# Attention and gated MLP on one core: low parts and reciprocals move to GpSimd, v without zero padding, the value product in three parts

## The chip, the cores and the metric

The kernel runs on one core of a Trainium2 chip. A core has TensorE (PE in the profile; its weight loads are PEld), VectorE (DVE), ScalarE (ACT), GpSimd (POOL) and SyncE (SP), which issues most DMAs. Each engine works through its own instructions in order and waits for others by semaphores. The metric is the device time of one execution in microseconds (us), the median of three runs.

## The reference

```python
# attention: q, k, v are (8, 12, 448, 64)
q_n, k_n = rmsnorm(q, g_q), rmsnorm(k, g_k)          # over the 64 of a head
scores = q_n @ k_n.T / sqrt(64)
attn = exp(scores - max(scores)); attn /= attn.sum(-1) + 1e-9
x = (attn @ v), heads joined: (8, 448, 768)
# gated MLP
h = gelu_tanh(x @ w_in)                              # (8, 448, 1024)
u, v2 = h[..., :512], h[..., 512:]
v_n = (v2 - mean) / sqrt(var + 1e-6) * g_ln          # over the 512
v_s = w_sg @ v_n + b_sg[:, None]                     # over the 448 positions
out = x + (u * v_s) @ w_out
```

## The kernel before

A number is carried through TensorE as two 16-bit halves, a high part and a low part (value minus high part), and a product is three matmuls: high by high, high by low, low by high. So for every operand someone makes the low part by a subtract.

The 96 heads of the 8 batches are taken in 48 pairs, and two pairs make a unit (24 units). The 448 positions are 3.5 tiles of 128, so a unit of two pairs has 7 tiles of queries; the middle one holds the last 64 positions of the first pair in its lower partitions and those of the second pair in its upper ones. The loop at the end of the kernel goes over the pairs. In each turn it prepares the next unit's q and k (squares, `norms`, `split`), makes the halves of this pair's v (`vsplit`), and then draws from generators in turn, by quotas: `scores` of the unit (quota SC), `pv` of the pair before (quota SV), the weights' preparation in the first 12 turns (quota WR), and `moe`, the MLP of the batch before (M0, M1, MR, ML). What a generator emits before it yields gets a place in the program; a scheduler then orders every engine's instructions from these places and its own estimate of times.

- `scores` (L409): per tile, TensorE makes the scores in PSUM (L423), DVE the negated row maximum (`nm`, L426), ACT two exponentials with row sums into the SBUF tile `ex` (L429), ACT the high part (L432) and DVE the low part (L433) of `ahl`, and SP transposes `ahl` into `at` by DMA (L438). After the middle and the last tile it calls `recips` (L380), which makes the reciprocals of the sums in two halves: four DVE instructions on 8 columns (`rx` L387, `ry` L388, `rh` L389, `rl` L390).
- `pv` (L445): `recip_row` (L392) spreads the reciprocals into a row by TensorE (L403), ACT copies it out (L406); then the value product is made in PSUM (L454, L459), DVE multiplies by the row (L461), ACT and DVE make the halves of x (L464, L465). The row and the product share one PSUM buffer.
- v is loaded for three pairs at once (`load_v`, L302, from SP's queue) into one of two buffers. The buffer has eight columns of 64 per pair, of which one half of two columns is zero, so that the step of the middle tile, 64 positions of either head, can be done by full 128x128 matmuls. `vsplit` makes the high part on ACT (L374) and the low part on DVE in one fused instruction, scale and subtract (L375).
- `split` (L327): GpSimd multiplies q and k by their weights and norms and subtracts for the low part (L334, L335, L340). In `moe` GpSimd gates (`gt`, L619) and makes low parts (`gl`, `gtl`).
- `weights` (L162): w_in and w_out come as 64-bit numbers and are decoded on DVE, ACT and GpSimd; DVE makes their low parts (L201, L247).
- `moe` (L488): `mv` and `mu` are the two halves of x @ w_in, `ms` is the product with w_sg, `mo` the one with w_out and the sum with x. `ms` is done for two feature tiles at a time (L601 to L624).

## Time and profile before

| | us |
|---|---|
| three runs | 1021.99, 1025.98, 1031.14; median 1025.98 |
| profiled execution | 1023.31, its span 1021.5 |
| DVE busy | 801.4 |
| ACT busy | 739.6 |
| GpSimd busy | 385.4 |
| PE busy by records | 826.5 |

Busy time is the time in which an engine has at least one instruction in work. Matmul records overlap, since the next one starts before the last has ended, so a busy PE has room left. The chain of work that ended last is followed back from the last instruction, at each step to what released it; its shares tell where the time was decided. An instruction's row names its line, operation, result and operands, its number, busy time and mean, and behind that the idle time of its engine in front of it and who ended it.

### The profile page before, as it was taken

Reading aid. Unit: us, or ns where it says so; the run is one execution under the profiler, and the core shown is the slowest. Engines: PE = TensorE matmul, PEld = TensorE weight load, DVE = VectorE, ACT = ScalarE, POOL = GpSimd, SP = SyncE. Lnnn points to the kernel's source line nnn. Section 1 sums busy time; section 2 is a strip of 40 time slices with the busy share of each in tenths; the row PEclk is TensorE's granted clock in tenths of the full one; section 3 lists DMA queues with packets and bytes.
Section 4 is the critical chain, followed back from the end, with each engine's and each line's share of the span. In section 5 each row is a group of like instructions: output and inputs, shape, how many; then the busy total and the mean of one; then the engine's idle time right before and its main releaser. Section 6 shows DMA issues by size and latency. Waiting matters only on the chain.

```text
span 1021.5 us, 16315 instructions
## 1 busy us (share of the span) xinstructions
PE 826.5 (81%) x5700; PEld 423.3 (41%) x5700; DVE 801.4 (78%) x1476; ACT 739.6 (72%) x1449; POOL 385.4 (38%) x263
## 2 busy tenths in 40 slices
PE   0324467737788899789897999989997899999998
PEld 0111224312553346344453455434643365445546
DVE  5699998999979977888789977887789768776140
ACT  2766798766777878686886877688778877786241
POOL 1465820436734362341543146322453253004021
PEclk9986678868989999899999899999998999999999
DMA  6977677776498869786789749793797676844102
GB/s 158 229 197 174 143 179 164 170 171 120 114 189 192 183 137 194 162 202 127 136 202 190 169 105 200 177 206 84 161 203 167 126 149 158 163 91 102 36 1 63
DMA packets 448002, 155.68 MB, mean 152 GB/s; under 512 B 404336, under 2 KB 441776, under 8 KB 447920
## 3 DMA queue, kind: packets, MB, share of 16 engines
q1 hardware_dynamic: 447344, 154.18, 69.3%
q8 instruction: 45, 0.74, 0.3%
q10 hardware_dynamic: 576, 0.46, 0.2%
q14 instruction: 37, 0.30, 0.1%
HBM read 43.57 MB, written 11.01 MB: 53 GB/s over the span
## 4 chain that ended last, share of the span: by engine, by line
DVE 31%; PE 28%; ACT 16%; DMA 10%; issue 9%; POOL 3%; SPq 3%; ACTq 0%; DVEq 0%; POOLq 0%
DVE ahl L433 8%; DMA at<-ahl 5%; DVE nm L426 5%; ACT ex L429 5%; ACT ahl L432 3%; PE s L423 3%; PE pv L459 3%; DVE vl L375 2%; DMA vr<-in_v_dram 2%; DVE ss L314 2%; DVE vl L568 1%; ACT sqv L358 1%; DVE pv L461 1%; DMA raw<-in_moe_w_in_dram 1%; SPq L302 1%
## 5 line engine op out<-in xcount | busy, mean ns | idle before, releaser
L429 ACT ACTIVATE ex<-s,nm 128x448 f32<-128x448 f32 x336 | 209.4, 631 | 76.8 <-DVE nm L426 51.6
L433 DVE TENSOR_TENSOR ahl<-ex,ahl 128x896 f16<-128x896 f32 x168 | 213.4, 1272 | 56.8 <-ACT ahl L432 55.4
L423 PE MATMUL s<-qt 64*128 64x448 f16 (+1 forms) x1152 | 156.9, 389 | 88.7 <-ACT ex L429 62.4
L426 DVE TENSOR_REDUCE nm<-s 128x2 f32<-128x896 f32 x168 | 180.8, 1081 | 18.4 <-PE s L423 18.2
L432 ACT ACTIVATE ahl<-ex 128x896 f16<-128x896 f32 x168 | 159.7, 951 | 37.8 <-DMA at<-ahl 35.8
L335 POOL TENSOR_TENSOR qk<-qk,ny 128x896 f32<-128x896 f32 x46 | 85.7, 1885 | 139.1 <-DVE ny L125 109.2
L619 POOL TENSOR_TENSOR gt<-gt,u 128x448 f32<-128x448 f32 x32 | 39.1, 1224 | 239.8 <-DVE gt L618 181.7
L340 POOL TENSOR_TENSOR hl<-qk,hl 128x896 f16<-128x896 f32 x46 | 94.6, 2070 | 69.9 <-ACT hl L339 69.7
L423 PEld LDWEIGHTS <-qt 64*128 64x128 f16 (+1 forms) x1152 | 49.2, 102 | 163.9 <-issue 102.8
L459 PE MATMUL pv<-at,vh 128*64 128x448 f16 x576 | 91.8, 371 | 0.0
L580 PEld LDWEIGHTS <-wi 128*128 128x128 f16 x576 | 57.6, 104 | 72.6 <-issue 31.3
L334 POOL TENSOR_TENSOR qk<-qk,gg 128x896 f32<-128x896 f32 x23 | 50.2, 2181 | 80.4 <-ACT sqk L313 78.2
L403 PE MATMUL row<-ident_h,rh 128*64 128x128 f16 (+1 forms) x384 | 36.6, 241 | 39.9 <-DVE xl L465 30.4
L429 ACT ACTIVATION_READ_ACCUMULATOR ex<-s,nm 128x1 f32 x336 | 67.8, 202 | 0.0
L314 DVE TENSOR_REDUCE ss<-sqk 128x14 f32<-128x896 f32 x48 | 51.6, 1076 | 17.6 <-ACT sqk L313 17.6
L313 ACT ACTIVATE sqk<-qk 128x896 f32<-128x896 f32 x48 | 45.6, 951 | 18.6 <-DVE ss L314 10.3
L339 ACT ACTIVATE hl<-qk 128x896 f16<-128x896 f32 x48 | 44.6, 945 | 13.6 <-POOL qk L335 6.9
L459 PE MATMUL pv<-at,vl 128*64 128x448 f16 x288 | 53.2, 367 | 0.0
L375 DVE SCALAR_TENSOR_TENSOR vl<-vr,v_s,vh 128x512 f16<-128x512 f32 x48 | 49.7, 1039 | 1.3 <-ACT vh L374 1.0
L459 PEld LDWEIGHTS <-vh 128*64 128x64 f16 x576 | 33.7, 114 | 40.5 <-issue 23.4
L403 PEld LDWEIGHTS <-rh 128*64 128x64 f16 (+1 forms) x384 | 22.5, 117 | 61.9 <-DVE xl L465 34.6
L522 PEld LDWEIGHTS <-xh 128*128 128x128 f16 x288 | 25.9, 99 | 46.8 <-issue 13.0
(1100 smaller groups left out, 2063.7 us busy)
## 6 DMA issues: line engine op xcount, KB each, us to landing
out_dram<-ot SPq DMA_DIRECT2D x56, 192.0 KB, 3.0
vr<-in_v_dram SPq DMA_DIRECT2D x32, 192.0 KB, 3.4
raw<-in_moe_w_in_dram SPq DMA_DIRECT2D x12, 512.0 KB, 5.5
qk<-in_q_dram SPq DMA_DIRECT2D x47, 128.0 KB, 2.9
qk<-in_k_dram SPq DMA_DIRECT2D x47, 128.0 KB, 2.8
...
```

The costliest lines, as they stand in the source:

```text
L314: V.tensor_reduce(out=SS[u][:, x], in_=skv, axis=AX.X, op=ALU.add)
L335: E.tensor_tensor(out=qk, in0=qk, in1=r["rs"][:, x * SSW:(x + 1) * SSW].unsqueeze(2).broadcast_to([P, SSW, D]), op=ALU.mult)
L340: E.tensor_tensor(out=l_, in0=r["qk"][:, x], in1=h_, op=ALU.subtract)
L375: V.scalar_tensor_tensor(out=vl.rearrange("p c d -> p (c d)"), in0=vr, scalar=sc, in1=vf, op0=ALU.mult, op1=ALU.subtract)
L403: mm(out=ps[h * HP:(h + 1) * HP, o:o + w], lhsT=rx[ks, 2 * n + h:2 * n + h + 1].broadcast_to([w, HP]), rhs=ident_h[ks, ks], start=(n == 0 ...
L423: mm(out=ps[r_, h, 0:S], lhsT=qt[hs, qx, t * P + r_.start:t * P + r_.stop], rhs=qt[hs, kx, j * S:(j + 1) * S], start=(m == 0), stop=(m == 2))
L426: V.tensor_reduce(out=nm, in_=ps[:, :, 0:S], axis=AX.X, op=ALU.max, negate=True)
L429: A.activation(out=ex[:, h], in_=ps[:, h, 0:S], func=AF.Exp, bias=nm[:, h:h + 1], accum_out=sums[:, t, h:h + 1])
L432: A.activation(out=ahl[:, 0], in_=ex, func=AF.Copy)
L433: V.tensor_tensor(out=ahl[:, 1], in0=ex, in1=ahl[:, 0], op=ALU.subtract)
L459: mm(out=ps[h * HP:(h + 1) * HP], lhsT=vx[:, c + h * (C4 + 1)], rhs=at_all[:, n + c + h * C4, o:o + S], start=False, stop=(c == CM - 1 and ...
L580: done = mm(out=ps[:, 0:S], lhsT=ww[:, g, f * P:(f + 1) * P], rhs=xx, start=(n == 0), stop=(n == 17))
```

## The change

The low part of v becomes two GpSimd instructions, a scaling in place in the load's buffer and a subtract; the low parts of w_in and w_out move to GpSimd as they are. `recips` is called by `pv` in place of `scores`, makes three of its four instructions on GpSimd (the reciprocal itself stays on DVE), and contains the row. v has seven columns and no zeros: the middle step of `pv` is done by pairs of 64x64 matmuls, first for all three products, and `pv` yields after 5 and after 9 of its 12 steps; its quota is 4 in place of 3. `ms` is done for one feature tile at a time, with the half tile last, and the first loop of `moe` yields after every second step also in the half tile. The exponentials are written to SBUF in both versions.

```diff
-SC, SV = 7, 3
+SC, SV = 7, 4
...
-            V.tensor_tensor(out=wi[:, t, 1], in0=tmp, in1=wi[:, t, 0], op=ALU.subtract)
+            G.tensor_tensor(out=wi[:, t, 1], in0=tmp, in1=wi[:, t, 0], op=ALU.subtract)
...
-            V.tensor_tensor(out=wo_l[:, t, es], in0=wr, in1=wo_h[:, t, es].bitcast(F32), op=ALU.subtract)
+            G.tensor_tensor(out=wo_l[:, t, es], in0=wr, in1=wo_h[:, t, es].bitcast(F32), op=ALU.subtract)
...
-    C8 = C7 + 1
-    vr_all = [ld.tile([P, GV, C8, D], F32, name=f"vr{n}", bufs=1) for n in range(NVR)]
-    for x in vr_all:
-        G.memset(x[hi, :, CM], 0.0)
-        G.memset(x[lo, :, C4], 0.0)
...
-        vr = vr_all[i // GV % NVR]
+        vr = ld.tile([P, GV, C7, D], F32, name="vr", bufs=NVR)
...
-        vh, vl = (att.tile([P, C8, D], F16, name="v" + c, bufs=NVH) for c in "hl")
+        vh, vl = (att.tile([P, C7, D], F16, name="v" + c, bufs=NVH) for c in "hl")
         vr = VR.pop(i)
         vf = vh.rearrange("p c d -> p (c d)")
         A.activation(out=vf, in_=vr, func=AF.Copy, scale=sc)
-        V.scalar_tensor_tensor(out=vl.rearrange("p c d -> p (c d)"), in0=vr, scalar=sc, in1=vf, op0=ALU.mult, op1=ALU.subtract)
+        G.tensor_scalar(out=vr, in0=vr, scalar1=sc, scalar2=None, op0=ALU.mult)
+        G.tensor_tensor(out=vl.rearrange("p c d -> p (c d)"), in0=vr, in1=vf, op=ALU.subtract)
...
-            if t in (CM, C7 - 1):
-                recips(NG * u + (t > CM))
             yield
...
     def recips(i):
...
-        V.tensor_scalar(out=x, in0=sums, scalar1=1e-9, scalar2=None, op0=ALU.add)
+        rh, rl = (sml.tile([P, 2 * C4], F16, name=f"r{c}", bufs=2) for c in "hl")
+        G.tensor_scalar(out=x, in0=sums, scalar1=1e-9, scalar2=None, op0=ALU.add)
         V.reciprocal(out=y, in_=x)
-        V.tensor_copy(out=rh, in_=y)
-        V.tensor_tensor(out=rl, in0=y, in1=rh, op=ALU.subtract)
+        G.tensor_copy(out=rh, in_=y)
+        G.tensor_tensor(out=rl, in0=y, in1=rh, op=ALU.subtract)
...
+        steps = [[(slice(0, P), c + h * C4) if c < CM else (slice(h * HP, (h + 1) * HP), CM) for h in range(2)]
+                 for c in range(C4)]
+        blocks = [(vx, n, hx) for vx, n in ((vh, 0), (vl, 0), (vh, C7)) for hx in steps]
+        blocks = blocks[CM::C4] + [x for n, x in enumerate(blocks) if n % C4 != CM]
+        row = recips(i)
         yield
-        row = recip_row(i)
         ps = ps_v.tile([P, 512], F32, name="pv")[:, 0:S]
-        parts = ((vh, 0), (vl, 0), (vh, C7))
-        for k_, (vx, n) in enumerate(parts):
-            mm(out=ps, lhsT=vx[:, CM:CM + 2].rearrange("p c d -> p (c d)"), rhs=at_all[:, n + CM, o:o + S],
-               start=(k_ == 0), stop=False, skip_group_check=True)
-        for c in range(CM):
-            for vx, n in parts:
-                for h in range(2):
-                    mm(out=ps[h * HP:(h + 1) * HP], lhsT=vx[:, c + h * (C4 + 1)], rhs=at_all[:, n + c + h * C4, o:o + S],
-                       start=False, stop=(c == CM - 1 and n == C7), skip_group_check=True)
+        for k_, (vx, n, hx) in enumerate(blocks):
+            for h, (ks, c) in enumerate(hx):
+                mm(out=ps[h * HP:(h + 1) * HP], lhsT=vx[ks, c], rhs=at_all[ks, n + c, o:o + S],
+                   start=(k_ == 0), stop=(k_ == len(blocks) - 1), skip_group_check=True)
+            if k_ in (4, 8):
+                yield
...
-            if st % 2 == 1 and (early or t != CM or g == NP - 1):
+            if st % 2 == 1:
                 yield
...
-        for f0 in range(2):
-            psf = {f: ps_m.tile([P, 512], F32, name="ms_", tag="mm") for f in (f0, f0 + 2)}
...
+        for f in range(FT):
+            ps = ps_m.tile([P, 512], F32, name="ms_", tag="mm")
+            n = 0
+            for t in range(CK):
...
+                for vx, wx in ((vh, ws_h), (vh, ws_l), (vl, ws_h)):
+                    mm(out=ps[:, 0:S], lhsT=vx[p0:p1, o:o + P], rhs=wx[p0:p1, t], start=(n == 0), stop=(n == 11))
+                    n += 1
+                if t == 1:
+                    yield
...
```

Three places show what the scheduler makes of it. The first is GpSimd's queue behind the gating of the second batch, before the change: `gl` and `gtl` are the MLP's, `hl` and `qk` the next unit's q and k.

```order
L622 TENSOR_TENSOR gl<-gt,gh 128x448
L623 TENSOR_TENSOR gtl<-gt,gh 128x64
L340 TENSOR_TENSOR hl<-qk,hl 128x2x7x64 x2
L334 TENSOR_TENSOR qk<-qk,gg 128x896
L335 TENSOR_TENSOR qk<-qk,ny 128x896 x2
L340 TENSOR_TENSOR hl<-qk,hl 128x2x7x64 x2
```

Some rows behind the same gating after the change: `rx`, `rh` and `rl` are the parts of the reciprocals, `vr` and `vl` the scaling and the low part of v.

```order
L330 TENSOR_TENSOR qk<-qk,ny 128x896 x2
L415 TENSOR_SCALAR rx<-sums 128x8
L335 TENSOR_TENSOR hl<-qk,hl 128x2x7x64
L417 CAST rh<-ry 128x8
L335 TENSOR_TENSOR hl<-qk,hl 128x2x7x64
L418 TENSOR_TENSOR rl<-ry,rh 128x8
L329 TENSOR_TENSOR qk<-qk,gg 128x896
L415 TENSOR_SCALAR rx<-sums 128x8
L417 CAST rh<-ry 128x8
L330 TENSOR_TENSOR qk<-qk,ny 128x896 x2
L418 TENSOR_TENSOR rl<-ry,rh 128x8
L370 TENSOR_SCALAR vr<-vr,v_s 128x448 x2
```

Between two instructions on q and k there now stand the parts of the reciprocals, and between these parts instructions on q and k of 896 columns.

The second place is DVE's queue in the middle of the run, before the change; `nm` and `ahl` are the scores' maxima and low parts, `nt` and `ny` belong to the norms of q and k, `xl` below is the low part of x.

```order
L124 TENSOR_TENSOR nt<-nt,ny 128x28
L387 TENSOR_SCALAR rx<-sums 128x8
L125 SCALAR_TENSOR_TENSOR ny<-nt,ny 128x28
L388 RECIPROCAL ry<-rx 128x8
L433 TENSOR_TENSOR ahl<-ex,ahl 128x896
L389 CAST rh<-ry 128x8
L390 TENSOR_TENSOR rl<-ry,rh 128x8
L461 TENSOR_TENSOR pv<-pv,row 128x448
L375 SCALAR_TENSOR_TENSOR vl<-vr_97,v_s,vh 128x512
```

And after it, at another such place:

```order
L393 TENSOR_REDUCE nm<-s 128x2 x2
L416 RECIPROCAL ry<-rx 128x8
L400 TENSOR_TENSOR ahl<-ex,ahl 128x896
L452 TENSOR_TENSOR pv<-pv,row 128x448
L400 TENSOR_TENSOR ahl<-ex,ahl 128x896
L456 TENSOR_TENSOR xl<-pv,xh 128x448
L393 TENSOR_REDUCE nm<-s 128x2 x2
```

On DVE one instruction of four is left, and it waits for GpSimd; a low part of `ahl` and the multiply of `pv` stand right behind it.

The third is TensorE in a middle batch. Before, the scores of a tile (L423) run through, and the value product begins with three full matmuls:

```order
L423 MATMUL s<-qt 128x448
L423 LDWEIGHTS qt
L423 MATMUL s<-qt 128x448
L454 LDWEIGHTS vh
L454 MATMUL pv<-at,vh 128x448
L454 LDWEIGHTS vl
L454 MATMUL pv<-at,vl 128x448
L454 LDWEIGHTS vh
L454 MATMUL pv<-at,vh 128x448
L459 LDWEIGHTS vh
L459 MATMUL pv<-at,vh 64x448
```

After, there are places at which the scores (L390, 64 rows of the array) alternate with the product with w_out (L646, 128 rows):

```order
L646 MATMUL mo__8109<-wo_h,gl 128x384
L390 LDWEIGHTS qt
L390 MATMUL s<-qt 128x448
L646 MATMUL mo__8109<-wo_h,gh 128x384
L390 LDWEIGHTS qt
L390 MATMUL s<-qt 128x448
L646 MATMUL mo__8109<-wo_l,gh 128x384
```

Each such alternation changes the array's shape, twice per pair. There are such places before the change too, but fewer.

More of the change, by code (lines that the diff above doesn't have):

```diff
@@ L438, in scores, with recips @@
                 nc.sync.dma_start_transpose(out=at_all[:, :, o1:o1 + r_.stop - r_.start], in_=src[r_])
-            if t in (CM, C7 - 1):
-                recips(NG * u + (t > CM))
             yield
+    def recips(i):
+        u, j = divmod(i, NG)
+        cs = slice(0, C4) if j == 0 else slice(CM, C7)
+        sums = U[u]["sums"][:, cs].rearrange("p t h -> p (t h)")
+        x, y = (sml.tile([P, 2 * C4], F32, name=f"r{c}", bufs=2) for c in "xy")
+        rh, rl = (sml.tile([P, 2 * C4], F16, name=f"r{c}", bufs=2) for c in "hl")
+        G.tensor_scalar(out=x, in0=sums, scalar1=1e-9, scalar2=None, op0=ALU.add)
+        V.reciprocal(out=y, in_=x)
+        G.tensor_copy(out=rh, in_=y)
+        G.tensor_tensor(out=rl, in0=y, in1=rh, op=ALU.subtract)
+        ps = ps_v.tile([P, 512], F32, name="row", tag="pv")[:, 0:S]
+        for n, t in enumerate(range(cs.start, cs.stop)):
+            ks, o = (slice(0, P), t * P - j * S) if t != CM else ((lo, SM), (hi, 0))[j]
+            for rx in (rh, rl):
+                for h in range(2):
+                    w = ks.stop - ks.start
+                    mm(out=ps[h * HP:(h + 1) * HP, o:o + w], lhsT=rx[ks, 2 * n + h:2 * n + h + 1].broadcast_to([w, HP]),
+                       rhs=ident_h[ks, ks], start=(n == 0 and rx is rh), stop=(n == CM and rx is rl), skip_group_check=True)
+        row = att.tile([P, S], F32, name="row", bufs=1)
+        A.activation(out=row, in_=ps, func=AF.Copy)
+        return row
     XT = {}
@@ L467, in pv @@
         del R[i]
-        yield
     def cluster(acts, done):
@@ L600, in moe @@
         bb = W["bb"]
-        for f0 in range(2):
-            psf = {f: ps_m.tile([P, 512], F32, name="ms_", tag="mm") for f in (f0, f0 + 2)}
-            for f, ps in psf.items():
-                n = 0
-                for t in range(CM):
-                    o = t * DH + f * P
-                    for vx, wx in ((vh, ws_h), (vh, ws_l), (vl, ws_h)):
-                        mm(out=ps[:, 0:S], lhsT=vx[:, o:o + P], rhs=wx[:, t], start=(n == 0), stop=False)
-                        n += 1
-                yield
-            for n, (vx, wx) in enumerate(((vh, ws_h), (vh, ws_l), (vl, ws_h))):
-                for f, ps in psf.items():
-                    p0, o = f // 2 * HP, CM * DH + f0 * P
-                    mm(out=ps[:, 0:S], lhsT=vx[p0:p0 + HP, o:o + P], rhs=wx[p0:p0 + HP, CM], start=False, stop=(n == 2))
-            for f, ps in psf.items():
-                gt = mlp.tile([P, S], F32, name="gt", tag="gt", bufs=NOT)
-                V.scalar_tensor_tensor(out=gt, in0=ps[:, 0:S], scalar=W["gw"][:, f:f + 1], in1=bb, op0=ALU.mult, op1=ALU.add)
-                G.tensor_tensor(out=gt, in0=gt, in1=u[f], op=ALU.mult)
-                A.activation(out=gh[:, f], in_=gt, func=AF.Copy)
-                gl[f] = mlp.tile([P, S], F32R, name="gl", tag="ug", bufs=5)
-                G.tensor_tensor(out=gl[f], in0=gt, in1=gh[:, f].bitcast(F32), op=ALU.subtract)
-                G.tensor_tensor(out=gtl[:, f, half], in0=gt[:, SM:S], in1=gh[:, f, SM:S].bitcast(F32), op=ALU.subtract)
@@ new lines, in moe @@
+        for f in range(FT):
+            ps = ps_m.tile([P, 512], F32, name="ms_", tag="mm")
+            n = 0
+            for t in range(CK):
+                p0, p1, o = 0, P, t * DH + f * P
+                if t == CM:
+                    p0 = f // 2 * HP
+                    p1, o = p0 + HP, t * DH + f % 2 * P
+                for vx, wx in ((vh, ws_h), (vh, ws_l), (vl, ws_h)):
[3 more added lines that the diff above has]
+                    yield
+            gt = mlp.tile([P, S], F32, name="gt", tag="gt", bufs=NOT)
+            V.scalar_tensor_tensor(out=gt, in0=ps[:, 0:S], scalar=W["gw"][:, f:f + 1], in1=bb, op0=ALU.mult, op1=ALU.add)
+            G.tensor_tensor(out=gt, in0=gt, in1=u[f], op=ALU.mult)
+            A.activation(out=gh[:, f], in_=gt, func=AF.Copy)
+            gl.append(mlp.tile([P, S], F32R, name="gl", tag="ug", bufs=5))
+            G.tensor_tensor(out=gl[f], in0=gt, in1=gh[:, f].bitcast(F32), op=ALU.subtract)
+            G.tensor_tensor(out=gtl[:, f, half], in0=gt[:, SM:S], in1=gh[:, f, SM:S].bitcast(F32), op=ALU.subtract)
```

28 lines of the change are left out of this document (3 added, 25 removed).

## The prediction

> **What bounds the kernel now.** I read the page first, for the shares of the engines and the chain of work that ended last, then three stretches of the span, then the groups by line, and last the timeline at a few places.
>
> ```profile
> PE 826.5 (81%) x5700; PEld 423.3 (41%) x5700; DVE 801.4 (78%) x1476; ACT 739.6 (72%) x1449; POOL 385.4 (38%) x263
> DVE 31%; PE 28%; ACT 16%; DMA 10%; issue 9%; POOL 3%; SPq 3%; ACTq 0%; DVEq 0%; POOLq 0%
> by line: issue 8.5%; DVE ahl L433 8.3%; DMA at<-ahl 4.8%; DVE nm L426 4.8%; ACT ex L429 4.7%; ACT ahl L432 3.1%; PE s L423 3.1%; PE pv L459 2.6%; DVE vl L375 2.2%; DMA vr<-in_v_dram 1.9%; DVE ss L314 1.6%; DVE vl L568 1.3%; ACT sqv L358 1.2
> ```
>
> Three engines are over 70% busy and none is full. The chain changes hands between DVE (31%) and PE (28%), so no single engine's time is the kernel's time; GpSimd (POOL) is the idle one, with 3% of the chain. The stretches separate the stages: up to 257 us the weights are decoded, up to 934 us attention and MLP overlap, and then the last batch's MLP runs out. The columns are busy us of PE, PEld, DVE, ACT and POOL with instruction counts, then the granted clock, the DMA share and GB/s.
>
> ```profile
> 0.00:257.00 257.00, 126.31 (x804) 54.47 (x805) 224.00 (x397) 180.22 (x347) 119.87 (x84) 0.81 0.74 171
> 257.00:934.00 677.00, 617.77 (x4380) 316.29 (x4380) 559.33 (x1034) 528.65 (x1051) 252.69 (x166) 0.96 0.75 159
> 934.00:1021.50 87.50, 82.45 (x520) 52.52 (x516) 18.08 (x47) 30.76 (x53) 12.88 (x15) 1.00 0.20 48
> ```
>
> DVE is first in the front (224 of 257), PE and DVE share the middle (618 and 559 of 677, ACT 529 close behind), and the tail is PE's alone (82 of 87.5).
>
> One more thing decides this case: some DVE work cannot run beside GpSimd work. The timeline at 544 us shows it.
>
> ```profile
> 544.71 0.17 DVE L387 TENSOR_SCALAR rx<-sums 128x8 f32<-128x8 f32 x1
> 545.15 2.58 DVE L433 TENSOR_TENSOR ahl<-ex,ahl 128x896 f16<-128x896 f32 x1
> 547.65 1.65 DVE L389 CAST rh<-ry 128x8 f16<-128x8 f32 x1
> 549.34 1.80 DVE L390 TENSOR_TENSOR rl<-ry,rh 128x8 f16<-128x8 f32 x1
> 545.10 4.18 POOL L335 TENSOR_TENSOR qk<-qk,ny 128x896 f32<-128x896 f32 x2 [10.62 <-DVE ny L125]
> 549.24 1.88 POOL L340 TENSOR_TENSOR hl<-qk,hl 128x896 f16<-128x896 f32 x1
> ```
>
> A subtract of 8 columns (L390) takes 1.80 us and ends at 551.14, just behind the GpSimd instruction that began 0.1 us before it and ended at 551.12. The rows of the whole run give the same: minimum, median and maximum of a duration.
>
> ```profile
> L433 DVE TENSOR_TENSOR ahl<-ex,ahl x168: 1040/1091/2777, 31.5 to 939.6; 128x896 f16<-128x896 f32 x168
> L375 DVE SCALAR_TENSOR_TENSOR vl<-vr,v_s,vh x48: 697/744/2408, 41.2 to 929.7; 128x512 f16<-128x512 f32 x48
> L389 DVE CAST rh<-ry x48: 156/170/1652, 42.5 to 939.1; 128x8 f16<-128x8 f32 x48
> L426 DVE TENSOR_REDUCE nm<-s x168: 1039/1080/1092, 24.7 to 936.1; 128x2 f32<-128x896 f32 x168
> ```
>
> The first three, whose operands lie in SBUF, wait up to the length of a GpSimd instruction; the maximum, read from PSUM (L426), never takes over 1.09 us. So to move work from DVE to GpSimd is not to move it out of DVE's way.
>
> **The change part by part.** The profiled execution took 1023.31 us, with a span of 1021.5; the median of the three runs is 1025.98. The sum is made on 1023.3. The groups by line that it needs (us busy, mean ns, idle before):
>
> ```profile
> L433 DVE TENSOR_TENSOR ahl<-ex,ahl 128x896 f16<-128x896 f32 x168 | 213.4, 1272 | 56.8 <-ACT ahl L432 55.4 <-ACT u L585 0.3
> L375 DVE SCALAR_TENSOR_TENSOR vl<-vr,v_s,vh 128x512 f16<-128x512 f32 x48 | 49.7, 1039 | 1.3 <-ACT vh L374 1.0
> L390 DVE TENSOR_TENSOR rl<-ry,rh 128x8 f16<-128x8 f32 x48 | 18.1, 376 | 0.7
> L389 DVE CAST rh<-ry 128x8 f16<-128x8 f32 x48 | 17.9, 374 | 0.6
> L387 DVE TENSOR_SCALAR rx<-sums 128x8 f32<-128x8 f32 x48 | 16.8, 349 | 11.8 <-ACT ex L429 11.4
> L201 DVE TENSOR_TENSOR wi<-tmp,wi 128x1024 f16<-128x1024 f32 x6 | 7.3, 1214 | 1.6 <-ACT wi L200 1.6
> L247 DVE TENSOR_TENSOR wo_l<-wr,wo_h 128x384 fp32r<-128x384 f32 x8 | 6.3, 786 | 0.0
> L340 POOL TENSOR_TENSOR hl<-qk,hl 128x896 f16<-128x896 f32 x46 | 94.6, 2070 | 69.9 <-ACT hl L339 69.7
> L619 POOL TENSOR_TENSOR gt<-gt,u x32: 1130/1134/2067, 249.6 to 995.2; 128x448 f32<-128x448 f32 x32
> L157 POOL TENSOR_SCALAR sqk<-sqk x12: 1488/1778/2212, 37.0 to 112.9; 128x512 f32<-128x512 f32 x12
> L157 POOL TENSOR_SCALAR sqo<-sqo x8: 1167/1182/1513, 177.2 to 233.7; 128x384 f32<-128x384 f32 x8
> L623 POOL TENSOR_TENSOR gtl<-gt,gh 128x64 fp32r<-128x64 f32 x32 | 18.1, 566 | 0.0
> ```
>
> Relief of DVE. Removed are 49.7 + 16.8 + 17.9 + 18.1 + 7.3 + 6.3 = 116 us; the reciprocal itself stays. On the chain of the last-ended work I can see 2.2% of 1021.5 = 22 us of vl, and among the longest pieces these (start, us):
>
> ```profile
> 88.04 1.44 DVE rh L389
> 204.20 2.40 DVE wo_l L247
> 271.08 1.59 DVE rh L389
> 332.18 1.48 DVE rx L387
> 337.14 1.75 DVE rl L390
> 547.73 1.58 DVE rh L389
> 763.02 1.71 DVE rx L387
> 764.99 1.39 DVE rh L389
> ```
>
> They add up to 13.3, with vl 36 us. That is the upper end of what can be won at once, and in the middle ACT, 559 - 529 = 31 us behind DVE, is next. The lower end is 0: nothing in the removal makes DVE slower. I take half of 36, -18: the pieces are mostly held ones, and another held instruction (ahl) stands behind each.
>
> What GpSimd takes on. The low part of v was one fused instruction and becomes two: a scaling in place of 448 columns, between 1.18 and 1.78 us by the medians for 384 and 512 columns, say 1.4, and a subtract of 448 at 1.13 as in L619. That is 48 x 2.5 = 120 us. Three instructions of 8 columns for each reciprocal lie between nothing and L623's 0.57 for 64 columns; at 0.25 they are 48 x 3 x 0.25 = 36. The weights' low parts take 6 x 2.2 (L340 scaled to 1024 columns is 2.4, less its waits) and 8 x 1.0, 21 us. GpSimd goes from 385 to about 560 us, 55% of the span. That hides if nobody waits for it, so the next three terms are about who does.
>
> Held ahl. The waits of L433 are now (1272 - 1091) x 168 = 30 us at 385 us of GpSimd. In proportion, 560 gives 44, so +14; by the chain's share of that line (8.3% of 1021.5 = 85 of 213, or 40%) +6. The bounds are 0 (the new instructions are short) and 14. The Trainium skill, GPSIMD Engine Reference, section 4.1, speaks against the change: elementwise work belongs on VectorE, GpSimd being about 2 times slower for two inputs. This trace makes it worse than that, 2.5 us against 0.74, since the fused form is split. By the page's factor vl would be an estimate of 48 x 2 x 0.74 = 71 us, and this term 4 instead of 6.
>
> Handovers. The reciprocal now waits on DVE for GpSimd's add, and everything queued on DVE, the maxima and ahl above all, waits behind it. With GpSimd busy 55% of the time and half an instruction of 1.8 us left on average, that is 0.5 us x 48 = 24 us. The lower bound is 0, where the add is always done in time. PE's own wait at the row is covered: counted over the order, 16 us of its work lie between a score tile and the row of its sums on average, against 12 before. I take 0.4 of 24, +10.
>
> The v chain. The next load of v goes into a buffer that now comes free after the two GpSimd instructions, and the load stands in SP's queue before transposes of ahl. Releases come about 2.5 - 1.0 + 0.5 = 2 us later. The chain has 1.9% of loads and 1.2% of their squares; eight of the sixteen loads on it at 2 us would be +16, none 0. I take +8. The batch's first vl has the same delay.
>
> TensorE. An array shape that differs from the one before costs time: the same product follows after 0.19 us, one of another shape after 0.28.
>
> ```profile
> 704.66 0.35 PE L608 MATMUL ms__7496<-ws_l,vh 128*128 128x448 f16 x1
> 704.85 0.35 PE L608 MATMUL ms__7496<-ws_h,vl 128*128 128x448 f16 x1
> 705.13 0.36 PE L615 MATMUL ms__7496<-ws_h,vh 64*128 64x448 f16 x1
> ```
>
> Counted over the order, shapes change 759 times now and 901 times after: 142 x 0.09 = 13 us, 1 of them in the tail. The paired 64x64 products of the unpadded v replace full ones one for one, so they cost nothing else. Besides, more products come behind the last score tile: 31 of 0.19, 8 of 0.18 and 12 of 0.06, together 8 us. The tail is PE's alone, so its 9 us count in full; of the middle's 12 - 8 = 4 I take half: +11, bounds 8 and 13. By the Trainium skill's opening page, Trainium Kernel Development and Optimization (Performance Expectations), matmul busy time is a bad metric and LDWEIGHTS busy share a good one; by 41% the middle would have room and the term would be 9.
>
> Edits with one answer: shorter v on ACT and four memsets less, -1; the yields and the quota of 4 only set the order, counted above. For exponentials nothing changes: they go to SBUF before and after.
>
> Sum: -18 + 6 + 10 + 8 + 11 - 1 = +16, so 1039 us. Its own range, 1028 to 1055, lets the halves vary.
>
> **The rivals.** It cancels. The handovers are in time and the v chain stays hidden: -18 + 6 + 11 - 1, with 2 each for the rest, is +2, so 1025. For it: GpSimd has 3% of the chain now. Against: 48 new waits on an in-order queue.
>
> Faster. DVE is what everything waits for, and the whole 36 us return, because the held instructions of the recips and vl, not ahl, were the late ones. With the handovers and the v chain hidden, -36 + 11 + 0 - 1 gives 997. It decides where DVE's queue reaches each reciprocal after GpSimd's add. For it: 31% of the chain, and 224 of 257 us in the front. Against: PE has more to do where it is already first.
>
> Much slower. GpSimd becomes a queue that others stand in: the upper bounds together, -18 + 14 + 24 + 16 + 13 - 1 = +48, so 1071. For it: the 10.62 us that L335 waited above; such a wait now holds recips and vl too. Against: 45% idle.
>
> **How the numbers follow.** The runs before spread over 0.9%, so 1% is what can be told from no change: 1016 to 1036. Forecast 0.38, of which 0.30 lies over 1036 and 0.08 within; cancelling 0.20; faster 0.26; much slower 0.16. So faster 0.26, same 0.28, slower 0.46. Cases of both signs hold the chance, so the range goes from 1000 to 1072; half of the faster and of the much slower case fall outside.
>
> **What would show it.** Relief: DVE's busy time falls from 801 to about 710 and the mean of L433's successor rises from 1272 to about 1350. Handovers: idle time before the reciprocal, released by GpSimd, of 10 to 25 us. v chain: v loads and squares above 3.1% of the chain. TensorE: start to start 0.28 at 901 changes, and a tail after the last score tile of 96 us instead of 87. I am wrong if DVE is idle before the reciprocal for less than 5 us, or if the middle stretch gets shorter.

## The result, and the profile after

The changed kernel takes 1041.85 us (median of four runs, 1040.59 to 1043.87), against 1025.68 for the kernel before on the same chip: a ratio of 1.0148, with a 95% interval of 1.0115 to 1.0181. It is slower by 1.5%. The forecast was 1039. The profiled execution took 1040.88 us, its span 1039.1, so it stands 18 us above the profiled execution of before.

The page of the kernel after, its first part (busy time, share, instructions) and the shares of the chain of work that ended last:

```profile
PE 841.7 (81%) x5844; PEld 430.7 (41%) x5844; DVE 744.2 (72%) x1270; ACT 737.0 (71%) x1451; POOL 592.6 (57%) x513
PE 35%; DVE 22%; ACT 13%; POOL 9%; DMA 8%; issue 8%; SPq 5%; POOLq 0%; ACTq 0%; DVEq 0%
```

DVE gave up 57 us of busy time and fell from 31% to 22% of the chain. GpSimd took on 207 us and went from 3% to 9%. The chain did not get shorter; it runs through TensorE (28% to 35%) and GpSimd instead. The groups by line of the same page (busy us, mean ns, idle before) show what became of the instructions in question:

```profile
L400 DVE TENSOR_TENSOR ahl<-ex,ahl 128x896 f16<-128x896 f32 x168 | 239.9, 1432 | 65.4 <-ACT ahl L399 64.9
L370 POOL TENSOR_SCALAR vr<-vr,v_s 128x448 f32<-128x448 f32 x48 | 78.5, 1637 | 61.4 <-ACT vh L369 53.1
L371 POOL TENSOR_TENSOR vl<-vr,vh 128x448 f16<-128x448 f32 x48 | 59.4, 1239 | 1.9
L415 POOL TENSOR_SCALAR rx<-sums 128x8 f32<-128x8 f32 x48 | 18.5, 384 | 98.8 <-ACT ex L396 96.7
```

The mean of `ahl` rose from 1272 to 1432 ns, though the instruction is the same. The same groups as minimum, median and maximum of a duration, and under the reciprocal the row of what ended DVE's idle time before it (us, times):

```profile
L400 DVE TENSOR_TENSOR ahl<-ex,ahl x168: 1031/1093/2993, 29.1 to 950.2; 128x896 f16<-128x896 f32 x168
L370 POOL TENSOR_SCALAR vr<-vr,v_s x48: 1397/1413/2358, 38.7 to 935.7; 128x448 f32<-128x448 f32 x48
L371 POOL TENSOR_TENSOR vl<-vr,vh x48: 1028/1037/1893, 41.6 to 937.2; 128x448 f16<-128x448 f32 x48
L415 POOL TENSOR_SCALAR rx<-sums x48: 233/248/1183, 38.4 to 949.8; 128x8 f32<-128x8 f32 x48
...
  POOL rx L415: 16.4, 17
```

An unheld `ahl` still takes 1.09 us; the surplus of the mean, (1432 - 1093) x 168 = 57 us, is waiting for GpSimd's instructions, against 30 us before. DVE stands idle in front of 17 of the 48 reciprocals, 16.4 us in all.

The stretches of the kernel after, cut at the first score matmul of the sixth unit and at the last score matmul of all (columns are PE, PEld, DVE, ACT, POOL busy, clock, DMA share, GB/s):

```profile
0.00:251.40 251.40, 119.34 (x755) 51.09 (x756) 199.66 (x333) 175.68 (x340) 169.17 (x135) 0.79 0.72 168
251.40:943.20 691.80, 631.62 (x4518) 322.37 (x4516) 523.01 (x890) 526.79 (x1055) 401.72 (x353) 0.96 0.75 158
943.20:1039.10 95.90, 90.78 (x573) 57.26 (x572) 21.56 (x47) 34.56 (x59) 21.70 (x27) 0.99 0.18 44
```

Before, the same two events lie at 255.7 and 934.2 us, close to the cuts that the prediction shows. So the front is 4 us shorter, the middle 13 us longer (678.6 to 691.8) and the tail 8.5 us longer (87.3 to 95.8): the whole loss lies behind the front. In the front DVE is relieved by some 24 us and GpSimd loaded by some 50; in the middle GpSimd goes from 253 to 402 us. The granted clock of the middle, the stretch that grew most, is 0.96 in both, so it does not carry these 13 us; what it may carry in other runs is taken up under what stays open.

### The profile page after: what moved, and what is told of

It reads as the page before. It is cut to its first block, busy times and chain, and to the rows that moved or that the text cites. A ratio compares the mean times of both kernels' runs of the same rounds, so it can differ in the third digit from the quotient of the medians.

```text
span 1039.1 us, 16765 instructions
## 1 busy us (share of the span) xinstructions
PE 841.7 (81%) x5844; PEld 430.7 (41%) x5844; DVE 744.2 (72%) x1270; ACT 737.0 (71%) x1451; POOL 592.6 (57%) x513
## 4 chain that ended last, share of the span: by engine, by line
PE 35%; DVE 22%; ACT 13%; POOL 9%; DMA 8%; issue 8%; SPq 5%; POOLq 0%; ACTq 0%; DVEq 0%
DVE ahl L400 6%; PE pv L448 5%; PE s L390 4%; ACT ex L396 4%; DMA at<-ahl 3%; DVE nm L393 3%; SPq L278 2%; ACT ahl L399 2%; POOL qk L330 2%; DVE ss L309 2%; POOL hl L335 2%; DMA raw<-in_moe_w_in_dram 2%; DMA vr<-in_v_dram 1%; POOL vr L370 1%; DMA qk<-in_q_dram 1%
## 5 line engine op out<-in xcount | busy, mean ns | idle before, releaser
L400 DVE TENSOR_TENSOR ahl<-ex,ahl 128x896 f16<-128x896 f32 x168 | 239.9, 1432 | 65.4 <-ACT ahl L399 64.9
L390 PE MATMUL s<-qt 64*128 64x448 f16 (+1 forms) x1152 | 166.5, 388 | 102.7 <-ACT ex L396 69.6
L390 PEld LDWEIGHTS <-qt 64*128 64x128 f16 (+1 forms) x1152 | 52.1, 102 | 176.3 <-issue 109.1
L448 PE MATMUL pv<-at,vh 128*64 128x448 f16 (+1 forms) x768 | 111.3, 377 | 4.3 <-ACT row L428 2.7
L370 POOL TENSOR_SCALAR vr<-vr,v_s 128x448 f32<-128x448 f32 x48 | 78.5, 1637 | 61.4 <-ACT vh L369 53.1
L335 POOL TENSOR_TENSOR hl<-qk,hl 128x896 f16<-128x896 f32 x46 | 92.5, 2023 | 32.6 <-ACT hl L334 32.4
L415 POOL TENSOR_SCALAR rx<-sums 128x8 f32<-128x8 f32 x48 | 18.5, 384 | 98.8 <-ACT ex L396 96.7
L448 PEld LDWEIGHTS <-vh 128*64 128x64 f16 (+1 forms) x768 | 41.3, 113 | 61.9 <-issue 40.7
L371 POOL TENSOR_TENSOR vl<-vr,vh 128x448 f16<-128x448 f32 x48 | 59.4, 1239 | 1.9
L448 PE MATMUL pv<-at,vl 128*64 128x448 f16 (+1 forms) x384 | 56.6, 375 | 1.6 <-POOL vl L371 1.6
```

What stands on the lines that cost most here:

```text
L335: E.tensor_tensor(out=l_, in0=r["qk"][:, x], in1=h_, op=ALU.subtract)
L370: G.tensor_scalar(out=vr, in0=vr, scalar1=sc, scalar2=None, op0=ALU.mult)
L371: G.tensor_tensor(out=vl.rearrange("p c d -> p (c d)"), in0=vr, in1=vf, op=ALU.subtract)
L390: mm(out=ps[r_, h, 0:S], lhsT=qt[hs, qx, t * P + r_.start:t * P + r_.stop], rhs=qt[hs, kx, j * S:(j + 1) * S], start=(m == 0), stop=(m == 2))
L400: V.tensor_tensor(out=ahl[:, 1], in0=ex, in1=ahl[:, 0], op=ALU.subtract)
L448: mm(out=ps[h * HP:(h + 1) * HP], lhsT=vx[ks, c], rhs=at_all[ks, n + c, o:o + S], start=(k_ == 0), stop=(k_ == len(blocks) - 1), skip_grou ...
```

## The experiments

The theory of the prediction: GpSimd's new work costs more than DVE's relief brings (held `ahl`, handovers, late v), and TensorE's new order adds its shape changes. Rivals: the order alone is the cause and the engines cancel; or the moves alone are the cause and the order is free. All times below are medians, all ratios are against the kernel before on the same chip with their 95% intervals; differences between two experiments are taken from the ratios, times 1026 us.

### The engine moves alone, and the rest alone

`x1_engines` is the kernel before with all of the engine moves and nothing else:

```diff
-            V.tensor_tensor(out=wi[:, t, 1], in0=tmp, in1=wi[:, t, 0], op=ALU.subtract)
+            G.tensor_tensor(out=wi[:, t, 1], in0=tmp, in1=wi[:, t, 0], op=ALU.subtract)
...
-            V.tensor_tensor(out=wo_l[:, t, es], in0=wr, in1=wo_h[:, t, es].bitcast(F32), op=ALU.subtract)
+            G.tensor_tensor(out=wo_l[:, t, es], in0=wr, in1=wo_h[:, t, es].bitcast(F32), op=ALU.subtract)
...
-        V.scalar_tensor_tensor(out=vl.rearrange("p c d -> p (c d)"), in0=vr, scalar=sc, in1=vf, op0=ALU.mult, op1=ALU.subtract)
+        G.tensor_scalar(out=vr, in0=vr, scalar1=sc, scalar2=None, op0=ALU.mult)
+        G.tensor_tensor(out=vl.rearrange("p c d -> p (c d)"), in0=vr, in1=vf, op=ALU.subtract)
...
-        V.tensor_scalar(out=x, in0=sums, scalar1=1e-9, scalar2=None, op0=ALU.add)
+        G.tensor_scalar(out=x, in0=sums, scalar1=1e-9, scalar2=None, op0=ALU.add)
         V.reciprocal(out=y, in_=x)
-        V.tensor_copy(out=rh, in_=y)
-        V.tensor_tensor(out=rl, in0=y, in1=rh, op=ALU.subtract)
+        G.tensor_copy(out=rh, in_=y)
+        G.tensor_tensor(out=rl, in0=y, in1=rh, op=ALU.subtract)
```

> Only the engine moves: low parts of v, w_in, w_out and three of the four reciprocal instructions on GpSimd, everything else as before (747 shape changes on TensorE in its order, 759 before). My sum: relief -18, held ahl +6, handovers +10, v chain +8, shapes -1: +5, so 1031. If TensorE's shapes and tail are all of the +16: 1025. If the engine moves are all of it: 1042.

Measured: 1032.98 us, 1.0052 (1.0028 to 1.0077), so +5.

`x2_order` is the kernel after with exactly these instructions back on DVE; the unpadded v, the new order of `pv` and `ms`, the place of `recips` and the quota stay:

```diff
-            G.tensor_tensor(out=wi[:, t, 1], in0=tmp, in1=wi[:, t, 0], op=ALU.subtract)
+            V.tensor_tensor(out=wi[:, t, 1], in0=tmp, in1=wi[:, t, 0], op=ALU.subtract)
...
-        G.tensor_scalar(out=vr, in0=vr, scalar1=sc, scalar2=None, op0=ALU.mult)
-        G.tensor_tensor(out=vl.rearrange("p c d -> p (c d)"), in0=vr, in1=vf, op=ALU.subtract)
+        V.scalar_tensor_tensor(out=vl.rearrange("p c d -> p (c d)"), in0=vr, scalar=sc, in1=vf, op0=ALU.mult, op1=ALU.subtract)
...
```

> Only the rest: v without padding, value product in three parts, reciprocals called by pv, ms one tile at a time, yields and quota, with all the moved instructions left on DVE (806 shape changes). My sum: shapes 47 x 0.09 = 4 plus up to 8 of tail: 1030 to 1038. If TensorE's part is all: 1031 or more, by its 806 changes less than the whole change. If the engine moves are all: 1026.

Measured: 1027.56 us, 1.0002 (0.9978 to 1.0025): no change. The order and the unpadded v by themselves cost nothing, although their shape changes on TensorE are 806 against 759. The two halves do not add up: 5 and 0, while the whole is 15. What the moves cost depends on the order in which they stand. The stretches of `x2_order`, cut by the same two events (its profiled execution, 1023.73 us, lies 4 below its median):

```profile
0.00:245.50 245.50, 120.91 (x796) 51.33 (x797) 210.24 (x382) 175.91 (x342) 111.59 (x74) 0.83 0.74 171
245.50:923.00 677.50, 616.48 (x4456) 316.90 (x4455) 557.85 (x1040) 521.22 (x1044) 248.75 (x162) 0.96 0.75 161
923.00:1021.90 98.90, 92.48 (x594) 58.25 (x592) 24.65 (x56) 38.37 (x65) 21.88 (x24) 0.99 0.20 47
```

Against these the kernel after is 6 us longer in the front, 14 us longer in the middle and 3 us shorter in the tail. So within the new order most of what the moves cost lies in the middle.

### Which of the moves

`x3_vl` moves only the low part of v, on the kernel before. `x9_rec_w` moves only the others: the three instructions of the reciprocals and the weights' low parts.

```diff
-        V.scalar_tensor_tensor(out=vl.rearrange("p c d -> p (c d)"), in0=vr, scalar=sc, in1=vf, op0=ALU.mult, op1=ALU.subtract)
+        G.tensor_scalar(out=vr, in0=vr, scalar1=sc, scalar2=None, op0=ALU.mult)
+        G.tensor_tensor(out=vl.rearrange("p c d -> p (c d)"), in0=vr, in1=vf, op=ALU.subtract)
```

> Of the change only the low part of v, on GpSimd in two instructions. My sum: half of 22 relief -11, two thirds of held ahl +4, v chain +8, 26 shape changes +2: 1029. If DVE's relief returns in full: 1012 to 1018. If GpSimd's work is in the way without any relief: 1038.

Measured: 1037.42 us, 1.0093 (1.006 to 1.0126): +10.

```diff
-            V.tensor_tensor(out=wi[:, t, 1], in0=tmp, in1=wi[:, t, 0], op=ALU.subtract)
+            G.tensor_tensor(out=wi[:, t, 1], in0=tmp, in1=wi[:, t, 0], op=ALU.subtract)
...
-            V.tensor_tensor(out=wo_l[:, t, es], in0=wr, in1=wo_h[:, t, es].bitcast(F32), op=ALU.subtract)
+            G.tensor_tensor(out=wo_l[:, t, es], in0=wr, in1=wo_h[:, t, es].bitcast(F32), op=ALU.subtract)
...
-        V.tensor_scalar(out=x, in0=sums, scalar1=1e-9, scalar2=None, op0=ALU.add)
+        G.tensor_scalar(out=x, in0=sums, scalar1=1e-9, scalar2=None, op0=ALU.add)
         V.reciprocal(out=y, in_=x)
-        V.tensor_copy(out=rh, in_=y)
-        V.tensor_tensor(out=rl, in0=y, in1=rh, op=ALU.subtract)
+        G.tensor_copy(out=rh, in_=y)
+        G.tensor_tensor(out=rl, in0=y, in1=rh, op=ALU.subtract)
```

> The kernel before with the reciprocals' three instructions and the weights' low parts on GpSimd, the low part of v left on DVE; 757 shape changes. The difference of x1_engines and x3_vl gives -4: 1022. By my sum (relief 7, handovers 10) 1029. If handovers cost nothing and the relief returns in full: 1010 to 1015.

Measured: 1026.35 us, 1.0015 (0.9985 to 1.0045): no change. The groups by line of this run:

```profile
L388 DVE RECIPROCAL ry<-rx 128x8 f32<-128x8 f32 x48 | 9.5, 198 | 14.6 <-POOL rx L387 13.8
L433 DVE TENSOR_TENSOR ahl<-ex,ahl 128x896 f16<-128x896 f32 x168 | 215.0, 1282 | 67.2 <-ACT ahl L432 66.6
```

The handovers are there, 13.8 us of idle DVE in front of the reciprocals, nearly the 16.4 of the kernel after, and the time is that of before. So this idle time lies off the path, or the relief of DVE pays for it; this run does not tell which. In the order of the kernel before, the reciprocals and the weights together cost nothing, and of the moves it is the low part of v that costs. These parts do not add up either: the low part of v alone costs 10, but beside the other moves only 4 (`x1_engines` against `x9_rec_w`), which their intervals do not tell from nothing.

### Relief and load of the low part of v, apart

`x6_load` is the kernel before, with DVE still making its low part; behind it GpSimd does the same two instructions once more, in the load's buffer, and nobody reads the result. It has the load without the relief, and it holds the buffer until DVE and GpSimd are both done.

```diff
         V.scalar_tensor_tensor(out=vl.rearrange("p c d -> p (c d)"), in0=vr, scalar=sc, in1=vf, op0=ALU.mult, op1=ALU.subtract)
+        G.tensor_scalar(out=vr, in0=vr, scalar1=sc, scalar2=None, op0=ALU.mult)
+        G.tensor_tensor(out=vr, in0=vr, in1=vf, op=ALU.subtract)
```

> The kernel before, with the two GpSimd instructions on v added behind DVE's own low part, which stays: nobody needs their result, they only load GpSimd and keep the buffer of v longer. DVE has no relief. My sum: held ahl +4, v chain +8, others held +3: 1040. Against x3_vl it shows the relief alone: by my sum x3_vl is 11 faster, by the cancelling case the two are equal.

Measured: 1055.31 us, 1.0261 (1.0229 to 1.0292): +27. Against `x3_vl` it is 17 us longer: that is what DVE's relief by this one instruction is worth here, together with the earlier release of the buffer, as far as two drawn orders can be compared.

The same extra load was put behind `x2_order`, once on a scratch tile that nobody else uses (`x7_free_load`), once in the v buffer (`x8_v_load`). The two differ in whether the next load of v waits for it.

```diff
+    dm = const.tile([P, S], F32, name="dm")
+    G.memset(dm, 1.0)
...
+        G.tensor_scalar(out=dm, in0=dm, scalar1=sc, scalar2=None, op0=ALU.mult)
+        G.tensor_tensor(out=dm, in0=dm, in1=dm, op=ALU.subtract)
```

> x2_order (1027.6, 806 changes) with two GpSimd instructions per pair on a scratch tile of 448 columns; no engine and no load of v waits for them, 796 changes. What it costs is GpSimd's work in the way alone: DVE instructions held, and q, k and gating later in GpSimd's queue. If the cost of x6_load (27 us) was mainly that: 1045 to 1055. If it was mainly the v buffer coming free late: 1030 to 1035.

Measured: 1037.2 us, 1.0116 (1.009 to 1.0143): +12 on `x2_order`, between the two cases that were expected.

```diff
+        G.tensor_scalar(out=vr, in0=vr, scalar1=sc, scalar2=None, op0=ALU.mult)
+        G.tensor_tensor(out=vr, in0=vr, in1=vf, op=ALU.subtract)
```

> x2_order with the same two instructions on the v buffer, after DVE's low part, so that the next load of v waits for them; 766 changes. Against x7_free_load it shows the wait of the v loads alone: by my term 8 us more than x7_free_load; if the v buffer is the main cost, 15 to 25 more; if it is hidden, the same.

Measured: 1019.27 us, 0.9944 (0.9923 to 0.9965): 6 us faster than `x2_order`, with more work. A buffer that comes free late is thus not enough to make a kernel slow. But the two runs differ in their order too (796 and 766 shape changes), so the pair does not price the buffer. It warns of something else: adding useless work made a kernel faster. The page of `x8_v_load`:

```profile
PE 821.1 (81%) x5844; PEld 427.0 (42%) x5844; DVE 807.2 (79%) x1476; ACT 732.5 (72%) x1449; POOL 525.2 (52%) x355
```

DVE is at 807 us and GpSimd at 525, both more than before, and the kernel is faster than before. Every edit here passes through the scheduler, which draws a new order for all engines; the next runs measure what that alone does.

### The order alone

Four kernels with the same instructions on the same engines as before or after, in another order. `x11_b_sv2` and `x12_b_sv5` are the kernel before with other quotas for `pv`, `x13_a_sv5` the kernel after.

```diff
-SC, SV = 7, 3
+SC, SV = 7, 2
```

> The kernel before with pv's quota at 2 instead of 3: the same instructions on the same engines in another order, with 867 shape changes instead of 759. If shape changes make the time: 108 x 0.09 = 10 more, 1036. If the order matters otherwise or not at all: anything near 1026, without regard to the count.

Measured: 1031.1 us, 1.0044 (1.0023 to 1.0064): +5, with 867 shape changes on TensorE.

```diff
-SC, SV = 7, 3
+SC, SV = 7, 5
```

> The kernel before with the quota at 5: the same instructions, 682 shape changes. If shape changes make the time: 77 x 0.09 = 7 less, 1019. If not: near 1026 or on either side.

Measured: 1026.03 us, 1.0002 (0.9979 to 1.0024): no change, with 682 shape changes.

```diff
-SC, SV = 7, 4
+SC, SV = 7, 5
```

> The changed kernel with the quota at 5 instead of 4: the same instructions, 810 shape changes instead of 901. If shape changes make the time: 91 x 0.09 = 8 less, 1034. If the changed kernel's slowness lies in its engine moves and not in the order: 1042.

Measured: 1043.55 us, 1.0158 (1.0128 to 1.0188), that of the kernel after, with 810 shape changes instead of 901.

`x10_a_mvms` is the kernel after with the old order inside the MLP: `ms` for two feature tiles at a time, and no yield at the half tile of the first loop.

```diff
-            if st % 2 == 1:
+            if st % 2 == 1 and (early or t != CM or g == NP - 1):
                 yield
...
-        for f in range(FT):
-            ps = ps_m.tile([P, 512], F32, name="ms_", tag="mm")
...
+        for f0 in range(2):
+            psf = {f: ps_m.tile([P, 512], F32, name="ms_", tag="mm") for f in (f0, f0 + 2)}
...
```

> The changed kernel with two edits undone: ms two feature tiles at a time again, and no yield in the half tile of moe's first loop. All engine moves stay; the order has 816 shape changes instead of 901. If the whole's slowness beyond x1_engines is TensorE's shape changes: 85 x 0.09 = 8 less, 1034. If it is the recips' late place or the unpadded v: 1042 as it was.

Measured: 1027.63 us, 1.0015 (0.9988 to 1.0043): 14 us less than the kernel after. Its page:

```profile
PE 831.5 (81%) x5844; PEld 428.8 (42%) x5844; DVE 738.3 (72%) x1270; ACT 737.8 (72%) x1451; POOL 591.8 (57%) x513
```

The instructions are the same in number, and DVE and GpSimd as busy as in the kernel after; only the order differs, and nearly all of the loss is gone. Shape changes do not explain it: they are 816 here, as in `x13_a_sv5` with its 810, which kept the whole loss. Taken together, 108 more changes came with +5 us, 77 fewer with 0, 91 fewer with +1, and 85 fewer with -14. By 0.09 us each they should have given +10, -7, -8 and -8.

### The low part of v, in the better order

`x14_a_mvms_vl` is `x10_a_mvms` with the low part of v on DVE again; the reciprocals and the weights stay on GpSimd.

```diff
-        G.tensor_scalar(out=vr, in0=vr, scalar1=sc, scalar2=None, op0=ALU.mult)
-        G.tensor_tensor(out=vl.rearrange("p c d -> p (c d)"), in0=vr, in1=vf, op=ALU.subtract)
+        V.scalar_tensor_tensor(out=vl.rearrange("p c d -> p (c d)"), in0=vr, scalar=sc, in1=vf, op0=ALU.mult, op1=ALU.subtract)
```

> x10_a_mvms (1027.6, 816 changes), which has every engine move, with the low part of v back on DVE in one instruction; 745 changes. If the low part of v costs 10 on GpSimd as x3_vl showed beside before: 1012 to 1018, of which 6 by shapes. If relief and load cancel: 1021 by shapes alone, or 1028.

Measured: 1002.98 us, 0.977 (0.9736 to 0.9805): 25 us less than `x10_a_mvms`, faster than both kernels and below every time that was expected of it. The first part of its page:

```profile
PE 826.4 (82%) x5844; PEld 427.9 (42%) x5844; DVE 761.6 (76%) x1318; ACT 733.1 (73%) x1449; POOL 461.2 (46%) x417
```

DVE is 23 us busier than in `x10_a_mvms` and the kernel 25 us faster. Where these come from is seen in the stretches by the same events as above. First `x10_a_mvms`, then `x14_a_mvms_vl`:

```profile
0.00:253.70 253.70, 120.15 (x760) 50.47 (x762) 199.38 (x333) 176.59 (x342) 170.32 (x136) 0.78 0.71 167
253.70:932.00 678.30, 617.31 (x4472) 319.03 (x4468) 515.59 (x887) 524.07 (x1049) 396.86 (x350) 0.95 0.76 161
932.00:1031.70 99.70, 94.05 (x618) 59.26 (x616) 23.30 (x51) 37.13 (x63) 24.65 (x29) 1.00 0.18 42
```

```profile
0.00:232.60 232.60, 114.27 (x736) 48.94 (x737) 195.91 (x329) 167.95 (x330) 146.18 (x113) 0.81 0.78 177
232.60:912.40 679.80, 622.61 (x4559) 322.23 (x4559) 545.13 (x944) 532.80 (x1065) 295.62 (x281) 0.95 0.75 162
912.40:1007.00 94.60, 89.53 (x550) 56.77 (x549) 20.51 (x47) 32.33 (x56) 19.41 (x25) 0.95 0.20 48
```

Both profiled executions lie 5.8 us above their medians, so they can be set against each other. They differ by 24.7 us, of which the front has 21.1 and the tail 5.1; the middle is 1.5 longer. In the middle GpSimd was relieved by 101 us and DVE loaded by 30, and the middle did not get shorter.

### What happens in the front

The stretch from 95 to 137 us in the kernel before, in the kernel after and in `x14_a_mvms_vl` (columns as above; of the busy times the fifth is GpSimd's, POOL):

```profile
95.00:137.00 42.00, 18.08 (x120) 7.50 (x120) 39.61 (x59) 32.44 (x62) 33.10 (x19) 0.62 0.77 171
```

```profile
95.00:137.00 42.00, 18.02 (x130) 7.82 (x130) 34.84 (x47) 31.11 (x68) 39.46 (x29) 0.62 0.68 155
```

```profile
95.00:137.00 42.00, 23.66 (x142) 9.28 (x141) 40.10 (x59) 36.27 (x76) 35.68 (x25) 0.60 0.81 177
```

GpSimd is busy 39.5 of 42 us in the kernel after; DVE, which was full before, now has 7 us to spare. Over the whole front GpSimd is less full, 169 of 251 us. The timeline of GpSimd in the kernel after, and what SP issues behind it:

```profile
104.91 2.08 POOL L329 TENSOR_TENSOR qk<-qk,gg 128x896 f32<-128x896 f32 x1
106.97 2.09 POOL L370 TENSOR_SCALAR vr<-vr,v_s 128x448 f32<-128x448 f32 x1
109.14 4.82 POOL L157 TENSOR_SCALAR sqk<-sqk 128x512 f32<-128x512 f32 x3
114.04 1.56 POOL L371 TENSOR_TENSOR vl<-vr,vh 128x448 f16<-128x448 f32 x1
115.56 3.79 POOL L158 TENSOR_TENSOR wi<-wi,sqk 128x512 f32<-128x512 f32 x2
...
130.46 1.88 POOL L335 TENSOR_TENSOR hl<-qk,hl 128x896 f16<-128x896 f32 x1
...
132.07 3.44 SPq L336 DMA_TRANSPOSE qt<-hl  x2
135.56 2.58 SPq L278 DMA_DIRECT2D qk<-in_q_dram  x4
138.18 3.54 SPq L278 DMA_DIRECT2D qk<-in_k_dram  x4
141.82 2.56 SPq L297 DMA_DIRECT2D vr<-in_v_dram  x4
```

And SP's timeline in `x14_a_mvms_vl`:

```profile
124.57 3.33 SPq L336 DMA_TRANSPOSE qt<-hl  x2
127.95 2.56 SPq L278 DMA_DIRECT2D qk<-in_q_dram  x4
130.56 2.56 SPq L278 DMA_DIRECT2D qk<-in_k_dram  x4
```

The two instructions of `vl`, 2.09 and 1.56 us here, stand in GpSimd's queue between the decode of the weights (`sqk`, `wi`) and the split of q and k (`qk`, `hl`). What comes behind them is later: the first `hl` is ready at 129.5 us instead of 122.0, its transposes start at 132.1 instead of 124.6, and SP's queue, which holds the next loads behind them, goes with it. GpSimd's queue is not shown to be all of it: in both kernels `hl` is ready 2.6 us before its transposes start, and these stand behind transposes of `ahl` in SP's queue. The end of the decode is later too. The loads of w_sg wait for the last low part of w_in (4.0 us in the kernel after, by its waits); first the kernel after, then `x14_a_mvms_vl` (minimum, median and maximum ns, first and last start in us):

```profile
L214 SPq DMA_DIRECT2D wsr<-in_moe_w_sg_dram x7: 497/594/1429, 167.2 to 171.7; - x7
```

```profile
L214 SPq DMA_DIRECT2D wsr<-in_moe_w_sg_dram x7: 497/594/595, 156.2 to 159.9; - x7
```

This start separates the fourteen kernels. The five in which GpSimd makes the low part of v have it at 167.2 (after), 167.2, 168.6, 169.6 and 172.7 us. The nine others have it between 156.2 and 165.0, and the latest of these is `x6_load`, with the same load for nothing. The first score matmul of the fifth unit separates them in the same way: 212.0 to 214.3 us in the five, 195.9 to 206.0 in the nine. GpSimd's load alone is not enough for it: in `x8_v_load` GpSimd is busy 36.5 of the same 42 us, and the start is 158.2. It goes with the low part of v, not with the weights' own: in `x9_rec_w` these are on GpSimd and the start is 161.3, in `x3_vl` they are on DVE and it is 169.6. How much of it reaches the end is another matter: `x10_a_mvms` and `x14_a_mvms_vl` lie 12.4 us apart in this start and 21.1 at the end of the front, while the kernel after begins its sixth unit 4 us before the kernel of before in spite of it. So the front is where `x14_a_mvms_vl` gains; it is not where the kernel after loses against the kernel before.

## Why the prediction was right, and where it was not

The time, the sign and the range were right: +16 was forecast and +16 measured. Neither sign of being wrong appeared: DVE is idle in front of the reciprocals for 16.4 us and not under 5, and the middle got longer. That the time was met so closely is luck, since not all of the terms were right and what moved the time as much as their sum is not among them.

**Relief of DVE, -18.** For the low part of v, 11 us were expected between `x6_load` and `x3_vl` and 17 measured, with the buffer's release and the order in them. For the reciprocals and the weights no relief was seen beside their cost: 0 in all, by `x9_rec_w`. DVE's busy time was put at about 710 us and is 744 (the terms, 801 less 116 and 14 more for `ahl`, give 699). Of the 116 us removed, 59 came back: 27 in `ahl`, the rest in other DVE instructions.

**Held `ahl`, +6.** The mechanism was right, the size too small. Its waits were put at 44 us and are 57, the mean at 1350 ns and is 1432. By the prediction's own share of 40% the 27 us more would be +11, inside its bounds. How much of these waits reaches the end was not measured apart.

**GpSimd's load, 560 us.** It is 593. The low parts of v were put at 120 us and take 138 (78.5 and 59.4), since their medians, 1.41 and 1.04 us, sum to 2.45, close to the forecast of 2.5, and the rest is time above the median. The reciprocals' parts, put at 36, take 57.5. The weights, put at 21, take 21. On the factor of about 2 that the Trainium skill gives for two inputs (GPSIMD Engine Reference, section 4.1): the subtract of two inputs takes 1.04 us, and the fused DVE instruction that it replaces, in `x14_a_mvms_vl`, 0.68, a factor of 1.5. The same section of the Trainium skill has one-input work on GpSimd at roughly line rate; here the one-input scaling with a scalar for each partition takes 1.41 us, longer than the subtract of the same 448 columns, so the measurement decides. The split form costs 3.6 times the fused one.

**Handovers, +10.** The idle time was forecast at 10 to 25 us and is 16.4. Its price, 0.4 of it, was neither shown nor refuted: `x9_rec_w` has 13.8 us of it, relieves DVE at the same time and takes the time of before. The terms' own sum for that run, 1029, lies inside its interval.

**The v chain, +8.** It did not show where the prediction looked for it: loads of v and their squares have 2.0% of the chain (14.9 and 5.8 us) instead of more than 3.1%. But the wait that the term names is there. In SP's queue the loads of v stand waiting for the low part of v, in the kernel before, in the kernel after and in `x10_a_mvms` (us in total, times, longest):

```profile
SPq L302 <- DVE vl L375: 4.1, 1, 4.1
```

```profile
SPq L297 <- POOL vl L371: 14.6, 9, 4.1
```

```profile
SPq L297 <- POOL vl L371: 5.5, 5, 2.3
```

Among the five kernels in which GpSimd makes the low part of v, this wait and the time rise together: 5.5 us in `x10_a_mvms` (+2), 10.5 in `x1_engines` (+5), 13.4 in `x3_vl` (+10), 14.6 in the kernel after (+15) and 15.7 in `x13_a_sv5` (+16). In the kernel after 12.5 of the 14.6 us lie in the middle, where most was lost. With one profiled execution of each this is a lead and no proof, and the wait does not rule alone: `x6_load` has 8.5 us of it and the longest time. The low part of v does cost, 10 us by `x3_vl` and 25 between `x10_a_mvms` and `x14_a_mvms_vl`, there for the most part in the front.

**TensorE, +11.** The tail was forecast at 96 us after the last score tile and is 95.8, and the 901 changes are there. But as a cause of the loss the term is not shown: `x2_order` and `x10_a_mvms` have more changes than before and longer tails (98.9 and 99.7 us), and take the time of before, `x2_order` with a front that is 10 us shorter. The price of 0.09 us for a change, read from two starts, does not carry over to the time of the whole, as the four orders above show. The share of weight loads is 41 or 42% in kernels of 1003, 1026, 1042 and 1055 us. The Trainium skill's opening page, Trainium Kernel Development and Optimization (Performance Expectations), holds it to be a good metric for how close a kernel is to roofline, the limit of the hardware; here it told none of the four apart.

**The step that was missing.** GpSimd's room was taken from the mean over the span, 55%. In the front, where the weights are decoded and DVE was first, it is 94% (39.5 of 42 us) in the stretch shown and 67% as a whole. The trace of before had the warning: 33.1 of 42 us in the same stretch, 79%, to which the new work was added. The rival that had GpSimd as a queue in which others stand named a mechanism that is seen, at a price, +48, that was too high. The front is not its only place: `vr` and `vl` have 18.4 us of the chain of the kernel after, and 17.0 of them lie behind the front.

**The sum.** Its terms were not measured one by one, and one cause is missing in it: the drawn order. That the order moves the time is shown by kernels of the same instructions: 1026, 1026 and 1031 us for before, 1028, 1042 and 1044 for after. So a forecast by terms of 5 to 10 us could be right to some 15 us at best, and of the +16 measured about as much hangs on the drawn order of the MLP's products (`x10_a_mvms`, -14) as on the engine moves (`x2_order`, -15). The two are not a sum: undoing the one gives -14, undoing `vl` as well gives another -25, while undoing all moves in the new order gives -15 in all.

**What stays open.** Why the order of `ms` costs the kernel after 14 us in its middle (691.8 us against 678.3) was not found; the counts of shape changes do not tell it, and the wait of the v loads, 14.6 us against 5.5, was not tested apart from the order. Nor was it settled why `x14_a_mvms_vl`, with the reciprocals and weights on GpSimd, beats `x2_order` by 24 us, when the same moves brought nothing to the kernel before.

The granted clock is a rival that no run separates from the rest. Within the kernel before, beside `x14_a_mvms_vl`, the slowest run took 1032.21 us at a clock of 0.914 and the fastest 1021.19 at 0.928; over the runs of before on three chips a fitted line gives 2 to 6 us for each 0.01. The means of the kernels differ by as much: 0.921 for before beside `x3_vl`, but 0.908 for `x3_vl`, 0.909 for `x6_load` and `x13_a_sv5`, 0.916 for the kernel after, 0.929 for `x2_order` and 0.932 for `x8_v_load`. By this estimate 3 to 8 of the 10 us of `x3_vl` go with the clock, and `x2_order` at the clock of before would be 2 to 5 us slower. Whether a lower clock makes these kernels slow, or a TensorE that waits more is granted less, is not shown. The comparison of `x10_a_mvms` with `x14_a_mvms_vl`, 0.920 and 0.921, is free of it.
